# Issuing the matmuls that spread token weights over expert slots before the first expert's tile

## The chip, the cores and the metric

The kernel runs on one core of a Trainium2 chip as one program. The metric is device time in microseconds (us): 409.35 us is the median of three runs, which lie between 408.04 and 410.41 us. Engines are named as in the profile: PE is the matmul engine and PEld its loading of weights, DVE the vector engine, ACT the scalar engine, POOL the GpSimd engine and SP the engine that issues most transfers.

## The reference

Three layers follow each other: chunked attention, a gated feed-forward layer that mixes positions, and a mixture of eight experts. Only the last one matters here:

```
logits     = x @ w_gate                       # [B, S, 8]
e[b, s]    = argmax of logits, or the expert of the token before it (by a local gate)
p[b, s]    = softmax(logits[b, s])[e]
out[b, s]  = p * (relu(x[b, s] @ w1[e]) @ w2[e])
```

There are 2 x 768 tokens of width 512, and each expert has 512 x 1024 weights in w1 and 1024 x 512 in w2. The weight p multiplies the finished row of a token, so it is wanted only when a tile of outputs is scaled.

## The kernel before

Tokens are sorted into columns of 128 slots, and a column belongs to one expert. The columns form units: unit 0 is column 0 alone, five "pairs" hold two columns each, and singles of one column stand between them; two singles are kept in quarters or halves of a column (`PART`). One unit is one object of the class `Unit`. Its steps are `gather` (rows of x fetched by an indirect transfer on POOL into `xg`), `xt` (transposes on PE into `xgp`, split into a high part `xe_h` on ACT and a low part `xe_l` on DVE), `l1` (PE, into `hp`), `relu`, `l2` (PE, into `op`), `out` (ACT scales `op` by `psl` at line 1325, POOL stores it). A weight chunk of 128 x 512 is loaded by SP as `raw` and split by `conv` into `we_h` (ACT, some on DVE) and `we_l` (DVE, line 210). Each matmul product of two split operands takes three passes.

Routing ends with four products on PE. `inv` gives the token of every slot, `eps` (line 1074, `tile_experts`, token `RE`) the expert of every column, `inv0` the tokens of unit 0. The fourth is `slots5`: 36 matmuls (12 token tiles by 3 parts of the weight, lines 1047 to 1051) of a 128 x 128 matrix `m` of zeros and ones and `s_mp` of 23 columns sum into one bank `psl`, and ACT copies that bank to the table `psl` of weights by slot (line 1052). `part_in` (line 1056) copies two of its columns on DVE.

The order of work up to the first expert's tile is written out by hand: `ORDER` is a list of tokens, each naming a generator that issues one step when its token comes up, and all five engines keep that order. Behind it `moe.run` issues the experts, and there PE and SP keep the order in which the code issues, while a scheduler places the work of ACT, DVE and POOL. In `run` (line 1385) unit 0 comes first: `l1(0)`, `l1(1)` cut by `ht_s(0)`, `l2(0)`, `T[1].xt()`, `l2(1)`, then the hook `extra` (line 1424), then its outputs; from there a loop takes unit j's `l1` and unit j-1's `l2` in turn. `feed` keeps loads 31 chunks ahead of PE and conversions `LC` = 12 chunks ahead.

Ahead of unit 0, `xt_late` (token `XL`, line 1178) builds its `xgp` from eight gathered rows and sixteen late products and splits it at once; `xe_h` of that split is what unit 0's first matmul reads. Unit 0's passes are sorted so that the eight products with `xe_h` come first.

Of the kernel before, what the change touches and what calls it, by code (L numbers as in the profile page):

```python
# [94 lines left out]
x13m2 RP RA x04h0 RP RP RP x12.2 R3 x13m3 RA RA RP RP RP RA RL RP R4 RA x02h0 RA x04h1 x04.1 x04.2 x13.1 x02h1 x02.1  # L95
RP RP x13.2 RP r5 r5 x10m0 x10m1 x10m2 x10m3 x02.2 x10.1 x05h0 x05h1 x14m0 x14m1 x14m2 cm5 cm6 RP RP x05.1 r7 x03.2 RP
RA RA RZ RO RP RP x10.2 RZ RP RP RP x05.2 r1 r1 x14m3 x15m0 x14.1 RS RS x15m1 x15m2 r3 x14.2 RT RT x15m3 x15.1 RT G0
XL RT XL XL RT x15.2 cm7 r6 RE RE RP XL G1 G2 RA
""".split()

ENG = dict(
# [15 lines left out]
def tile_kernel(  # L117
# [269 lines left out]
    class Tr:  # L387
# [10 lines left out]
        def at(self, w, k, t0, n):  # L398
            g, o = divmod(t0, 256)
            return self.t[g, k // 2][w][:, (k % 2) * 256 + o : (k % 2) * 256 + o + n]  # L400
# [326 lines left out]
    RT = []  # L727
# [756 lines left out]
    moe = Moe([[0], *units, *singles[PU - 1 :]])  # L1484
# [86 lines left out]
    for name, fn, *a in (  # L1571
        ("R1", route1, 1, lx[1]), ("R2", route2, 1), ("R3", route3, 1), ("R4", route4, 1),
        ("RM", ranks_mm, 1), ("RA", rank_all), ("RP", place_ops), ("RZ", slots0), ("RS", slots3),
        ("RL", late_rows), ("RO", rows1, 1), ("RT", slots4), ("RE", tile_experts),
        ("G0", moe.T[0].gather, True), ("G1", moe.T[1].gather), ("G2", moe.T[2].gather),
        ("XL", lambda: (yield from moe.T[0].xt_late(xs[1][TT - LATE :]))),
    ):
        at(name, fn, *a)
    moe.extra, moe.later = slots5, {3: part_in, 5: part_out}

    live = {}

# [116 lines left out]
```

## Time and profile before

| | us |
|---|---|
| median of three runs | 409.35 |
| the profiled execution | 407.93 |
| its span from first to last instruction | 406.2 |
| PE busy | 394.1 (97% of the span) |
| DVE busy | 311.0 (77%) |
| ACT busy | 191.9 (47%) |
| POOL busy | 40.4 (10%) |

Times of a row are counted from the start of the span. A matmul's row has a start and a modelled end, and the starts of matmuls that follow each other lie closer together than a matmul is long (0.23 us against 0.39 us for 512 columns), so a matmul's price in a stream is the distance of two starts. In brackets behind a row stands the idle time of the engine ahead of it and who ended it.

### The profile page before, as it was taken

The page shows a single profiled execution, that of the slowest core. Times are in us where ns is not written, and L with a number is a line of the kernel's source. Part 1 is how long each engine was busy: PE and PEld are TensorE (multiplying, and loading weights), DVE is VectorE, ACT ScalarE, POOL GpSimd, SP SyncE. Part 2 cuts the span into 40 slices and gives each one's busy share as a digit, 9 for nine tenths or more (in the row PEclk, how much of TensorE's full clock was granted, in tenths as well). Part 3 has the DMA queues.
Part 4 walks back from the last instruction along what each step waited for, and adds up shares of the span by engine and source line. Part 5 has one row for each costly group of instructions (what it writes and reads, how often), then busy time and mean ns, then how long its engine had stood idle before and what let it go on. Part 6 is the DMA issues. An engine that isn't in the chain of part 4 may idle for free. (4 is left out here: it accounts for less than half of the span.)

```text
span 406.2 us, 9418 instructions
## 1 busy us (share of the span) xinstructions
PE 394.1 (97%) x3466; PEld 343.5 (85%) x3466; DVE 311.0 (77%) x749; ACT 191.9 (47%) x429; POOL 40.4 (10%) x58
## 2 busy tenths in 40 slices
PE   8979999999999999999999999999999999999994
PEld 4667899999999999996687789889888968978983
DVE  2989999999889988889799886996896684545400
ACT  4989885625454312520211265755683562643401
POOL 1000000020020010000000232101230210100201
PEclk9999999999999999999999999999999999999999
DMA  7999996100001032000074299999998599870101
GB/s 232 341 348 351 344 350 228 55 26 2 2 2 52 2 130 79 2 2 0 32 280 157 83 330 390 392 343 330 384 396 303 175 303 388 283 267 2 45 3 45
DMA packets 43703, 75.98 MB, mean 187 GB/s; under 512 B 5925, under 2 KB 12977, under 8 KB 43650
## 3 DMA queue, kind: packets, MB, share of 16 engines
q1 hardware_dynamic: 39682, 65.41, 46.8%
q0 software_dynamic: 2240, 6.75, 4.5%
q10 hardware_dynamic: 1728, 3.15, 2.0%
q8 instruction: 29, 0.48, 0.5%
q14 instruction: 24, 0.20, 0.2%
HBM read 68.99 MB, written 6.75 MB: 186 GB/s over the span
## 5 line engine op out<-in xcount | busy, mean ns | idle before, releaser
L210 DVE TENSOR_TENSOR we_l<-raw,we_h 128x512 fp32r<-128x512 f32 x128 | 82.1, 687 | 18.8 <-ACT we_h L205 18.1
L205 ACT ACTIVATE we_h<-raw 128x512 fp32r<-128x512 f32 x105 | 59.0, 625 | 17.2 <-DVE s_y L968 12.4
L1230 PE MATMUL hp<-xe_h,we_h 128*128 128x256 f32 x160 | 45.4, 284 | 0.0
L1230 PE MATMUL hp<-xe_h,we_l 128*128 128x256 f32 x160 | 44.9, 281 | 0.0
L1230 PE MATMUL hp<-xe_l,we_h 128*128 128x256 f32 x160 | 44.9, 281 | 0.0
L1313 PE MATMUL op<-we_h,ht_h 128*128 128x512 f32 x104 | 41.8, 402 | 0.0
L1313 PE MATMUL op<-we_l,ht_h 128*128 128x512 f32 x104 | 41.0, 394 | 0.0
L1313 PE MATMUL op<-we_h,ht_l 128*128 128x512 f32 x104 | 41.0, 394 | 0.0
L684 PE MATMUL vsp<-sg_h,vh_h 128*128 128x256 f32 x144 | 41.0, 285 | 0.0
L684 PE MATMUL vsp<-sg_l,vh_h 128*128 128x256 f32 x144 | 40.5, 281 | 0.0
L684 PE MATMUL vsp<-sg_h,vh_l 128*128 128x256 f32 x144 | 40.4, 280 | 0.0
L1230 PEld LDWEIGHTS hp<-xe_h,we_h 128*128 128x128 f32 x160 | 30.1, 188 | 0.1
L1230 PEld LDWEIGHTS hp<-xe_l,we_h 128*128 128x128 f32 x160 | 30.2, 188 | 0.0
L1230 PEld LDWEIGHTS hp<-xe_h,we_l 128*128 128x128 f32 x160 | 30.1, 188 | 0.0
L1262 DVE SCALAR_TENSOR_TENSOR ht_l<-hp,ht_h 128x512 fp32r<-128x512 f32 x20 | 13.8, 691 | 18.0 <-ACT ht_h L1261 18.0
L684 PEld LDWEIGHTS vsp<-sg_h,vh_h 128*128 128x128 f32 x144 | 27.1, 188 | 0.2 <-issue 0.2
L655 PE MATMUL ups<-x_h,in_h 128*128 128x256 f32 x96 | 27.2, 283 | 0.0
L684 PEld LDWEIGHTS vsp<-sg_h,vh_l 128*128 128x128 f32 x144 | 27.1, 188 | 0.0
L684 PEld LDWEIGHTS vsp<-sg_l,vh_h 128*128 128x128 f32 x144 | 27.1, 188 | 0.0
L655 PE MATMUL ups<-x_h,in_l 128*128 128x256 f32 x96 | 27.0, 281 | 0.0
L655 PE MATMUL ups<-x_l,in_h 128*128 128x256 f32 x96 | 27.0, 281 | 0.0
L469 ACT ACTIVATE a<-sc,nm 128x96 f32<-128x96 f32 x96 | 24.0, 385 | 2.5 <-DVE nm L466 2.5
(275 smaller groups left out, 930.5 us busy)
## 6 DMA issues: line engine op xcount, KB each, us to landing
raw<-in_w SPq DMA_DIRECT2D x160, 256.0 KB, 5.7
v<-in_vw SPq DMA_DIRECT2D x23, 260.0 KB, 5.3
k<-in_kw SPq DMA_DIRECT2D x24, 192.0 KB, 4.9
raw_in<-in_w_in SPq DMA_DIRECT2D x16, 256.0 KB, 5.6
q<-in_qT SPq DMA_DIRECT2D x12, 256.0 KB, 4.7
x1d<-x ACTq DMA_DIRECT2D x12, 256.0 KB, 2.1
rsg<-in_w_sgT SPq DMA_DIRECT2D x9, 256.0 KB, 4.4
raw_out<-in_w_out SPq DMA_DIRECT2D x8, 256.0 KB, 5.2
```

The lines of the kernel that those rows point to most:

```text
L205: nc.scalar.activation(hi, src, AF.Copy)
L210: nc.vector.tensor_tensor(lo, src, hi.bitcast(F32), ALU.subtract)
L469: nc.scalar.activation(self.a[:, j, :], sc[:, j, :], AF.Exp, bias=nm[:, j : j + 1])
L655: nc.tensor.matmul(ps[:, i * 256 : (i + 1) * 256], win_u[k][wa][:, f * 128 : (f + 1) * 128], xT[self.b].at(wb, k, 256 * self.g, 256), star ...
L684: nc.tensor.matmul(self.ps[:, h * 256 : (h + 1) * 256], self.vh[s].hl[wa][:, f * 128 : (f + 1) * 128], rhs_sg(wb, s, self.g), start=(s == ...
L1230: nc.tensor.matmul(ps[:, i * 256 : (i + 1) * 256], self.w[f // 4 * 4 + k][wa][:, f % 4 * 128 : (f % 4 + 1) * 128], self.x[k // 2][wb][:, k ...
L1262: nc.vector.scalar_tensor_tensor(l, self.ps[s], 0.0, h.bitcast(F32), ALU.max, ALU.subtract)
L1313: nc.tensor.matmul(self.po[c], h[wa][:, o : o + 128], self.w[8 + k][wb], start=(k == 0 and n == 0), stop=(k == 7 and n == 2),)
```

## The change

The token `R5` for `slots5` is entered in `ORDER` behind the last `XL` and ahead of `G1` and `G2`, the gathers of units 1 and 2, and the hook `extra` is no longer set. The 36 matmuls and the copy are the same ones.

```
-XL RT XL XL RT x15.2 cm7 r6 RE RE RP XL G1 G2 RA
+XL RT XL XL RT x15.2 cm7 r6 RE RE RP XL R5 G1 G2 RA
...
-        ("RL", late_rows), ("RO", rows1, 1), ("RT", slots4), ("RE", tile_experts),
+        ("RL", late_rows), ("RO", rows1, 1), ("RT", slots4), ("RE", tile_experts), ("R5", slots5),
...
-    moe.extra, moe.later = slots5, {3: part_in, 5: part_out}
+    moe.later = {3: part_in, 5: part_out}
```

On PE, between the last product of `eps` and unit 0's first matmul, stood before:

```order
L1074 MATMUL eps<-s_eqj,r0e 1x23
L1253 MATMUL hp<-we_h,xe_h 128x512
L1253 MATMUL hp<-we_l,xe_h 128x512
L1253 MATMUL hp<-we_h,xe_h 128x512
L1253 MATMUL hp<-we_l,xe_h 128x512
```

and the last of the 36 products stand there now:

```order
L1049 MATMUL psl<-s_mp_3675,m_3610 128x23
L1049 LDWEIGHTS m_3610
L1049 MATMUL psl<-s_mp_3676,m_3610 128x23
L1253 MATMUL hp<-we_h,xe_h 128x512
L1253 MATMUL hp<-we_l,xe_h 128x512
```

So all 36 have moved in between `eps` and `hp`.

On PE, between unit 0's `l2` and the first `l1` of unit 1 (`hp` with 256 columns), the end of the 36 stood before:

```order
L1049 MATMUL psl<-s_mp_3675,m_3610 128x23
L1049 LDWEIGHTS m_3610
L1049 MATMUL psl<-s_mp_3676,m_3610 128x23
L1230 MATMUL hp<-xe_h,we_h 128x256
L1230 MATMUL hp<-xe_l,we_h 128x256
```

and now `l2` meets `l1` directly:

```order
L1313 MATMUL op<-we_h,ht_h 128x512
L1313 MATMUL op<-we_l,ht_h 128x512
L1313 MATMUL op<-we_h,ht_l 128x512
L1230 MATMUL hp<-xe_h,we_h 128x256
L1230 MATMUL hp<-xe_l,we_h 128x256
```

On ACT, from the split of unit 0's `xgp` to the relu of unit 1's first `hp`, stood before:

```order
L205 ACTIVATE xe_h<-xgp 128x512
L205 ACTIVATE we_h<-raw 128x512 x3
L1266 ACTIVATE hr<-hp 128x512
L205 ACTIVATE ht_h<-htp 128x512
L205 ACTIVATE we_h<-raw 128x512 x3
L1266 ACTIVATE hr<-hp 128x512
L205 ACTIVATE ht_h<-htp 128x512
L205 ACTIVATE we_h<-raw 128x512 x3
L205 ACTIVATE xe_h<-xgp 128x512 x2
L1052 COPY psl<-psl 128x23
L205 ACTIVATE we_h<-raw 128x512 x2
L1261 ACTIVATE ht_h<-hp 128x512
```

and now:

```order
L205 ACTIVATE xe_h<-xgp 128x512
L1052 COPY psl<-psl 128x23
L205 ACTIVATE we_h<-raw 128x512 x3
L1266 ACTIVATE hr<-hp 128x512
L205 ACTIVATE ht_h<-htp 128x512
L205 ACTIVATE we_h<-raw 128x512 x3
L1266 ACTIVATE hr<-hp 128x512
L205 ACTIVATE ht_h<-htp 128x512
L205 ACTIVATE we_h<-raw 128x512 x3
L205 ACTIVATE xe_h<-xgp 128x512 x2
L205 ACTIVATE we_h<-raw 128x512
L1261 ACTIVATE ht_h<-hp 128x512
```

The copy has moved ahead of three conversions and the first `hr`. On DVE the two copies of `part_in` move with it:

```order
L210 TENSOR_TENSOR xe_l<-xgp,xe_h 128x512
L1056 COPY s_part<-psl 128x1 x2
L207 CAST we_h<-raw 128x512
L210 TENSOR_TENSOR we_l<-raw,we_h 128x512 x4
L210 TENSOR_TENSOR ht_l<-htp,ht_h 128x512
```

They now stand behind the `xe_l` of unit 0, where before they stood behind those of unit 1. POOL and SP issue the same instructions in the same order as before.

## Rows read from the trace of the kernel before

**Rows 1.** The page: engines' busy time; PE and its clock in 40 slices.
```profile
PE 394.1 (97%) x3466; PEld 343.5 (85%) x3466; DVE 311.0 (77%) x749; ACT 191.9 (47%) x429; POOL 40.4 (10%) x58
...
PE   8979999999999999999999999999999999999994
...
PEclk9999999999999999999999999999999999999999
```

**Rows 2.** Waits by engine and line over the span, PE's: total, times, longest.
```profile
PE xp L503 <- DMA v<-in_vw: 1.6, 3, 1.0
...
PE hp L1253 <- ACT xe_h L205: 0.3, 1, 0.3
```

**Rows 3.** Windows: stretch, length, busy time of PE, PEld, DVE, ACT, POOL; clock; DMA.
```profile
230.40:231.20 0.80, 0.50 (x14) 0.34 (x13) 0.52 (x3) 0.65 (x2) 0.00 (x0) 1.00 0.13 44
...
245.30:400.00 154.70, 154.70 (x1038) 133.25 (x1035) 97.27 (x168) 77.85 (x147) 23.93 (x23) 1.00 0.74 261
```

**Rows 4.** Timeline of PE at the end: start, us, instruction.
```profile
400.00 0.40 PE L1313 MATMUL op<-we_h,ht_l 128*128 128x512 f32 x1
```

**Rows 5.** Timeline of PE round the place where the products stand before.
```profile
244.11 0.39 PE L1313 MATMUL op<-we_h,ht_l 128*128 128x512 f32 x1
244.35 1.07 PE L1049 MATMUL psl<-s_mp,m 128*128 128x23 bf16 x36
245.27 0.36 PE L1230 MATMUL hp<-xe_h,we_h 128*128 128x256 f32 x1
245.47 0.28 PE L1230 MATMUL hp<-xe_l,we_h 128*128 128x256 f32 x1
245.59 0.28 PE L1230 MATMUL hp<-xe_h,we_l 128*128 128x256 f32 x1
```

**Rows 6.** Timeline of PE where one stream of products meets another.
```profile
263.40 0.40 PE L1253 MATMUL hp<-we_h,xe_l 128*128 128x512 f32 x1
263.64 0.40 PE L1313 MATMUL op<-we_h,ht_h 128*128 128x512 f32 x1
263.88 0.39 PE L1313 MATMUL op<-we_l,ht_h 128*128 128x512 f32 x1
```

**Rows 7.** Timeline of PE round the place where the products go.
```profile
230.44 0.45 PE L1074 MATMUL eps<-s_eqj,r0e 128*1 128x23 f16 x12
231.20 0.50 PE L1253 MATMUL hp<-we_h,xe_h 128*128 128x512 f32 x1 [0.30 <-ACT xe_h L205]
```

**Rows 8.** Timeline of DVE from the products' inputs to unit 1's split.
```profile
228.83 0.79 DVE L1040 TENSOR_TENSOR s_mp<-s_eqj,s_pp 128x276 bf16<-128x276 f16 x2
...
231.30 0.67 DVE L210 TENSOR_TENSOR xe_l<-xgp,xe_h 128x512 fp32r<-128x512 f32 x1
...
236.74 0.69 DVE L210 TENSOR_TENSOR ht_l<-htp,ht_h 128x512 fp32r<-128x512 f32 x1 [1.90 <-ACT ht_h L205]
...
243.69 1.28 DVE L210 TENSOR_TENSOR xe_l<-xgp,xe_h 128x512 fp32r<-128x512 f32 x2
245.66 0.21 DVE L1056 COPY s_part<-psl 128x1 f32<-128x1 f32 x2 [0.69 <-ACT psl L1052]
```

**Rows 9.** Timeline of ACT from unit 0's split to the copy and behind it.
```profile
230.55 0.60 ACT L205 ACTIVATE xe_h<-xgp 128x512 fp32r<-128x512 f32 x1 [0.60 <-PE xgp L1188]
231.04 1.66 ACT L205 ACTIVATE we_h<-raw 128x512 fp32r<-128x512 f32 x3
234.34 0.60 ACT L1266 ACTIVATE hr<-hp 128x512 f32<-128x512 f32 x1 [1.63 <-PE hp L1253]
...
245.45 0.18 ACT L1052 COPY psl<-psl 128x23 f32<-128x23 f32 x1 [2.82 <-PE psl L1049]
245.53 1.16 ACT L205 ACTIVATE we_h<-raw 128x512 fp32r<-128x512 f32 x2
248.41 0.60 ACT L1261 ACTIVATE ht_h<-hp 128x512 fp32r<-128x512 f32 x1 [1.73 <-PE hp L1230]
```

**Rows 10.** Waits of SP's queue over the span, at the loads of chunks.
```profile
SPq L1139 <- DMA raw<-in_w: 14.6, 24, 1.4
SPq L1139 <- DVE we_l L210: 11.7, 13, 6.3
```

## The prediction

> **What bounds the kernel now.** I read the page first: PE is busy for 97% of the span, with no slice but the last under 0.7, and its granted clock is full in all 40 slices [rows 1]. The next question is whether PE paces itself or waits. The waits of PE over the whole span are short, and only one lies near the change: unit 0's first matmul, which waits 0.3 us for `xe_h` [rows 2]. The windows agree: in the 0.80 us up to 231.20 PE is busy for 0.50 us, whereas from 245.30 to 400.00 it is busy for all 154.70 us [rows 3]. From there the chain runs through PE's last matmul, which starts at 400.00 [rows 4], then one scaling and one store, to the end at 406.2. So a microsecond that PE saves before 245 reaches the end, unless a smaller delay on ACT, DVE or SP comes to light behind it.
>
> **What is removed.** At the old place the 36 products start at 244.35 and the next matmul starts at 245.27: 0.92 us, or 0.026 us each [rows 5]. There is a second, smaller piece. The first matmul behind them takes 0.20 us to the next start, where the third comes 0.12 us after the second, so 0.08 us is lost where the bf16 products hand over to the split ones [rows 5]. Where one stream of split products meets another, the distance stays as it was: 263.40, 263.64, 263.88 [rows 6]. Without the 36, `l2` meets `l1` in that way, so I count the 0.08 us as gone too; by the other bound it stays. Removed: 0.92 to 1.00 us.
>
> **What is added.** At the new place the twelve `eps` products start at 230.44. Their row spans 0.45 us from the first start to the last end; at the spacing of the 36, 0.026 us, the next product could start at 230.44 + 12 x 0.026 = 230.75. The matmul that follows starts only at 231.20, since ACT's `xe_h` runs from 230.55 to 231.15 [rows 7, 9]. So 0.45 us of PE's time is free there (the 0.30 us in brackets is less because it counts from a modelled end). The 36 then run from 230.75 to 231.67, and unit 0 starts at 231.67 instead of 231.20: 0.47 us later. Its wait for `xe_h` is covered by the products, and what is late next is nothing on PE: `xe_l` ends at 231.97 [rows 8], and it is wanted only by the ninth matmul of unit 0, some two microseconds in. The handover of 0.08 us costs nothing new here, since `eps` already hands over to split products at this point.
>
> The inputs of the products are ready: the last two of the three `s_mp` end at 229.62 [rows 8], 1.1 us before PE gets there. If this cover were gone, PE would stand in front of unit 0 for as long as `s_mp` is late.
>
> **The sum on PE.** -1.00 + 0.47 = -0.53 us by the time unit 1's `l1` has passed the handover; -0.45 us if the handover stays.
>
> **What must hold between the two places.** Three chains run along unit 0, and each is moved by the change.
>
> ACT: the copy stands now ahead of three conversions. In the trace the copy starts 0.21 us after the start of the last product (245.27 - 0.03 = 245.24 to 245.45), and the conversion behind it 0.08 us after the copy [rows 5, 9]. So at the new place the copy starts at about 231.85, and the conversions at 231.93 instead of 231.04: 0.89 us late. What is queued behind is those three and `hr`, for which PE waits at its next transposes. ACT sat idle for 1.63 us before `hr` [rows 9], and `hr` itself is wanted 0.47 us later than before, so 1.63 + 0.47 - 0.89 = 1.2 us of cover is left, and nothing is paid. Further on ACT gains: the 2.82 us of waiting for the products, with two conversions queued behind, disappear [rows 9]. PE waits for no conversion there, so I count the gain at nothing; the most that it could be worth is a PE wait that no row shows.
>
> The Trainium skill ("TensorE: Matmul & The Clock Gate", section "Architectural detail: the array is 16× 32×32, not 1× 128×128") states that ACT and DVE take their queues strictly in order. That speaks against the change, since a copy that waits holds everything behind it. This trace agrees: the conversion at 245.53 stood behind the waiting copy [rows 9]. By the rule the hold is the 0.89 us above, and if ACT could pass a waiting instruction it would be nothing; with 1.2 us of cover left the sum is the same with both, and the rule decides only the rival below.
>
> DVE: the two `s_part` copies (0.21 us together) now stand ahead of a cast and four conversions and wait for ACT's copy until 232.1. They finish at about 232.3, where DVE before went on at 231.90. The 0.4 us are absorbed by the 1.90 us of idle time before `ht_l` at 236.74 [rows 8].
>
> DVE again, and here it is tight. From 236.74 to 244.97 DVE works without a gap, up to unit 1's two `xe_l` [rows 8]. This run starts with `ht_h`, which follows PE, so it shifts by PE's 0.47 us: the first `xe_l`, which ends at 243.69 + 0.68 = 244.37 (half of the pair's 1.28 us plus the overlap of two that follow each other), now ends at 244.84. ACT's `xe_h` releases PE 0.05 us after its end (231.15 to 231.20) [rows 7, 9]; by that PE may read `xe_l` from 244.89. PE itself now starts unit 1 at 244.35 + 0.47 = 244.82 and wants the first `xe_l` one matmul later, at 244.94. That leaves 0.05 us, and if the wait takes hold at the weights' load, which comes ahead of the matmul by about one distance of 0.12 us, PE is held by 0.07 us. So the gain lies between 0.45 and 0.53 us; I take 0.5.
>
> SP and POOL issue the same things in the same order. The loads of unit 1's chunks follow PE's releases by at most the 0.47 us, and conversions run twelve chunks ahead of PE: at 12 matmuls of 0.12 us to a chunk of a pair [rows 5] that is 17 us of work, and at three of 0.23 us to a chunk of a single [rows 6] it is 8 us.
>
> **Forecast.** 407.93 - 0.5 = 407.4 us against the profiled execution. That execution lies 1.42 us under the median of the runs shown; set on the median, the time is 409.35 - 0.5 = 408.85, say 408.8 us. That is 0.12%, far below the 0.5% (2.05 us) that a measurement of this kernel can tell from no change: its own three runs lie 2.37 us apart. The mechanism has 80% of my chance.
>
> **Rival 1: the gain is eaten before unit 1.** If the hold of ACT goes through to `ht_h` in full, DVE's unbroken run shifts by 0.89 us, the first `xe_l` ends at 245.26, and unit 1's second matmul can go at 245.31 instead of 245.47. The gain is then 0.16 us: 409.2 us. For it speaks that DVE has no gap in 8.2 us [rows 8]; against it, that 1.63 us of idle time lies ahead of `hr` and 1.90 us ahead of `ht_l` [rows 8, 9]. It would need a hold of over 2.1 us. The lower bound of this rival is no gain at all, 409.35, where the stall at 231.20 gives no cover. 12%.
>
> **Rival 2, slower: chunks come later.** The products' inputs are five buffers of the pool of 86 (two `m`, three `s_mp`) out of which every later chunk takes its buffer too. They come free 13.6 us earlier on PE, so the buffers are dealt out differently to the loads that follow, and such a load waits for whichever reader its buffer had last. In the trace the longest of these waits is 6.3 us, for a `we_l` [rows 10]. Two such waits in a row, 12.6 us, against the 8.4 us of conversions ahead at the singles would leave PE standing for 4.2 us: 409.35 - 0.5 + 4.2 = 413.05 us. It decides from about 8.4 us of lateness on. Against it: five buffers that come free earlier let loads go out earlier as a rule, and not one microsecond of PE behind 245.30 is idle [rows 3], so the stock of chunks never ran out. 4%.
>
> **Rival 3: more than the sum.** ACT's earlier conversions might let loads and later splits run ahead and take away short stalls that hide under the modelled ends of matmuls. Four such stalls of 0.5 us would be needed to get past 0.5%: 406.8 us. No row shows them. 4%.
>
> That the change doesn't do what it says is out: the order of instructions shows all 36 and the copy at the new place.
>
> **How the numbers follow.** Faster by over 0.5%: rival 3 and a little for scatter, 0.05. Slower by over 0.5%: rival 2 and a little for scatter, 0.05. Within: 0.90. The range is the forecast with the scatter of the runs shown, 1.3 us below their median and 1.1 us above, and reaches rival 1: 407.3 to 410.4 us. Rival 2 lies outside it.
>
> **What would show it.** In the changed profile `psl` should run from about 230.75 to 231.67 with no wait before unit 0's first `hp`; that `hp` should start about 1.2 us after the first `eps`, not 0.76 us; `l2` of unit 0 should meet unit 1's `hp` with no 0.08 us of handover; ACT's `hr` should still have idle time before it; and from unit 1's first matmul to PE's last the distance should be the 154.7 us of before. The prediction is wrong if that distance changes by over half a microsecond, if PE waits for `xe_l` or for a chunk behind unit 0, or if the products are slower than 0.026 us each at their new place.

## The result, and the profile after

The changed kernel takes 412.25 us (median of six runs, 410.98 to 413.45) where the kernel before takes 408.94 (six runs, 408.04 to 410.41): a ratio of 1.0073, 95% interval 1.0050 to 1.0096. It is slower by about 3 us. The forecast was 408.8 us, and 412.25 lies outside its range of 407.3 to 410.4. The profiled execution of the changed kernel takes 411.96 us, with a span of 410.2.

The page's rows for PE and its clock, which answer to [rows 1]: as many busy microseconds as before, at full clock, in a longer span.

```profile
PE 394.2 (96%) x3466; PEld 343.0 (84%) x3466; DVE 311.0 (76%) x749; ACT 192.5 (47%) x429; POOL 40.4 (10%) x58
...
PE   8888999999999999999999989899999999999994
...
PEclk9999999999999999999999999999999999999998
```

So PE waits. Its waits by line (total, times, longest) now hold two behind 230 us that [rows 2] don't have, and the wait for `xe_h` at unit 0 is gone:

```profile
PE op L1313 <- ACT ht_h L205: 1.6, 1, 1.6
PE hp L1253 <- DVE xe_l L210: 1.3, 1, 1.3
```

The windows (stretch, length, busy time of PE and the others) answer to [rows 3]. The new place is filled; the 5.2 us round unit 0's first `op` hold 1.64 us of idle time; and from unit 1's first matmul to PE's last there are 156.43 us instead of 154.7, with 1.25 us idle.

```profile
230.76:232.06 1.30, 1.30 (x49) 1.25 (x49) 1.02 (x5) 0.60 (x1) 0.00 (x0) 1.00 0.06 19
236.00:241.20 5.20, 3.56 (x16) 2.07 (x15) 1.07 (x2) 2.12 (x5) 1.90 (x2) 1.00 0.91 282
247.73:404.16 156.43, 155.18 (x1035) 133.27 (x1033) 97.65 (x168) 77.08 (x145) 23.96 (x23) 1.00 0.72 253
```

PE's timeline at the new place and at the old one (start, duration, instruction; answers to [rows 5, 7]):

```profile
230.76 0.45 PE L1074 MATMUL eps<-s_eqj,r0e 128*1 128x23 f16 x12
231.14 1.07 PE L1049 MATMUL psl<-s_mp,m 128*128 128x23 bf16 x36
232.06 0.48 PE L1253 MATMUL hp<-we_h,xe_h 128*128 128x512 f32 x1
...
247.50 0.40 PE L1313 MATMUL op<-we_h,ht_l 128*128 128x512 f32 x1
247.73 0.28 PE L1230 MATMUL hp<-xe_h,we_h 128*128 128x256 f32 x1
247.85 0.35 PE L1230 MATMUL hp<-xe_l,we_h 128*128 128x256 f32 x1
248.04 0.29 PE L1230 MATMUL hp<-xe_h,we_l 128*128 128x256 f32 x1
```

The products went where they should and cost what they should. The loss begins behind them. PE's and ACT's timelines of the changed kernel:

```profile
236.48 0.66 PE L1279 MATMUL htp<-ident,hr 128*128 128x128 f32 x4
236.89 0.48 PE L1253 MATMUL hp<-we_h,xe_h 128*128 128x512 f32 x1
237.21 0.39 PE L1253 MATMUL hp<-we_l,xe_h 128*128 128x512 f32 x1
237.44 1.07 PE L1253 MATMUL hp<-we_h,xe_l 128*128 128x512 f32 x4
240.15 0.51 PE L1313 MATMUL op<-we_h,ht_h 128*128 128x512 f32 x1 [1.64 <-ACT ht_h L205]
```
```profile
235.83 0.60 ACT L1266 ACTIVATE hr<-hp 128x512 f32<-128x512 f32 x1 [1.81 <-PE hp L1253]
239.50 0.60 ACT L205 ACTIVATE ht_h<-htp 128x512 fp32r<-128x512 f32 x1 [3.08 <-PE hp L1253]
```

The four transposes `htp` end at 237.14, ACT is idle, and nothing stands ahead of `ht_h`; still it starts only at 239.50. In the kernel before, `ht_h` starts at 236.11 behind transposes that end at 236.08:

```profile
235.48 0.60 PE L1279 MATMUL htp<-ident,hr 128*128 128x128 f32 x4
```
```profile
236.11 0.60 ACT L205 ACTIVATE ht_h<-htp 128x512 fp32r<-128x512 f32 x1 [1.17 <-PE htp L1279]
```

In the changed trace PE's semaphore for these transposes is updated at 239.476, and the three updates behind it follow at 239.52, 239.55 and 239.60, though the matmuls that they belong to started at 237.21, 237.44 and 238.12. PE had worked; its reports came late and in a bunch. SP's queue too took 0.73, 0.69 and 0.73 us over three instructions between 237.21 and 239.40; instructions of these kinds take 0.05 to 0.46 us at that place of the kernel before. What runs on POOL then are gathers, first in the changed kernel, then in the kernel before:

```profile
234.88 0.95 POOL L1176 DMA_INDIRECT xg<-x1d,gidx  x1 [0.30 <-issue]
236.14 0.95 POOL L1176 DMA_INDIRECT xg<-x1d,gidx  x1 [0.30 <-issue]
237.39 0.95 POOL L1176 DMA_INDIRECT xg<-x1d,gidx  x1 [0.30 <-issue]
```
```profile
236.01 0.95 POOL L1176 DMA_INDIRECT xg<-x1d,gidx  x1 [0.30 <-PE hp L1253]
237.26 0.95 POOL L1176 DMA_INDIRECT xg<-x1d,gidx  x1 [0.30 <-issue]
```

The last two (unit 3's, the fourth and fifth of a row of five) start 0.53 us behind the first transpose in the kernel before, and 0.34 us ahead of it in the changed one. Counted from the first `eps` product the transposes have moved back by 0.69 us (5.03 to 5.72), and the fourth gather has come forward by 0.19 us (5.57 to 5.38).

The second stall is of the same make. Unit 1's third `ht_h` (line 1261) waits 3.21 us for PE, while unit 4's and 5's gathers run; `xe_h` and `xe_l` of unit 2 stand behind it on ACT and DVE, and PE waits for the latter. ACT, POOL and DVE of the changed kernel:

```profile
258.99 0.60 ACT L1261 ACTIVATE ht_h<-hp 128x512 fp32r<-128x512 f32 x1 [3.21 <-PE hp L1230]
259.48 0.62 ACT L205 ACTIVATE we_h<-raw 128x512 fp32r<-128x512 f32 x1
260.00 0.59 ACT L205 ACTIVATE xe_h<-xgp 128x512 fp32r<-128x512 f32 x1
```
```profile
255.21 0.98 POOL L1176 DMA_INDIRECT xg<-x1d,gidx  x1 [0.30 <-issue]
256.50 0.99 POOL L1176 DMA_INDIRECT xg<-x1d,gidx  x1 [0.30 <-issue]
257.79 0.94 POOL L1176 DMA_INDIRECT xg<-x1d,gidx  x1 [0.30 <-issue]
```
```profile
261.89 0.68 DVE L210 TENSOR_TENSOR xe_l<-xgp,xe_h 128x512 fp32r<-128x512 f32 x1
```

Where the time went, as the distance in us from the first `eps` product to PE's start of each step (the last column is an experiment below, the changed kernel with five gathers held back):

| PE starts | before | changed | changed, both holds |
|---|---|---|---|
| unit 0's first hp | 0.76 | 1.31 | 1.31 |
| unit 0's first htp | 5.03 | 5.72 | 5.55 |
| unit 0's first op | 6.86 | 9.39 | 7.38 |
| unit 1's first hp | 14.82 | 16.97 | 14.41 |
| unit 2's first hp | 27.54 | 29.89 | 27.07 |
| the op behind it | 33.20 | 37.10 | 32.72 |
| the last matmul | 169.56 | 173.40 | 169.07 |

### The profile page after: what moved, and what is told of

Its sections match the earlier page's. It is cut to its first block, busy times and chain, and to the rows that moved or that the text cites. A ratio compares the mean times of both kernels' runs of the same rounds, so it can differ in the third digit from the quotient of the medians.

```text
span 410.2 us, 9414 instructions
## 1 busy us (share of the span) xinstructions
PE 394.2 (96%) x3466; PEld 343.0 (84%) x3466; DVE 311.0 (76%) x749; ACT 192.5 (47%) x429; POOL 40.4 (10%) x58
## 5 line engine op out<-in xcount | busy, mean ns | idle before, releaser
L1313 PEld LDWEIGHTS op<-we_h,ht_h 128*128 128x128 f32 x104 | 19.5, 188 | 7.5 <-ACT ht_h L205 2.1
```

Source lines behind the costliest of these rows:

```text
L1313: nc.tensor.matmul(self.po[c], h[wa][:, o : o + 128], self.w[8 + k][wb], start=(k == 0 and n == 0), stop=(k == 7 and n == 2),)
```

## The experiments

Several theories were put to the test. **G**: POOL's gathers hold up PE's reports for one to two microseconds, and the change moves unit 0's transposes into such a stretch. **S**: the five slot buffers that come free early re-deal the buffers of loads and gathers. **A1** and **A2** (or P): ACT's copy in front of unit 0, or the products themselves. Ratios are to the kernel before on the same chip, with 95% intervals.

**The two kernels once more.**

> The changed kernel once more, to see whether its two stalls of PE (1.8 us before unit 0's first op matmul at 238.1, 1.3 us before a pair's hp at 261.0) stand at the same places in another execution. Theory A (the change itself makes PE report finished matmuls late near unit 0, so that ACT's ht_h starts 2 to 3 us late and PE waits for it): time 411 to 413 us, both stalls again at the same instructions, ACT's ht_h again over 2 us behind the end of the transposes. Theory B (the profiled execution was disturbed, and the loss sits elsewhere): time still 411 to 413 us, but the stalls stand at other instructions or are missing. Theory C (there is no real loss): time within 0.5% of the kernel before, 407 to 411 us.

> The kernel before, profiled once more. Theory A: 408 to 410 us, PE without a wait of 0.5 us or more between 231 and 400 us, and ACT's ht_h of unit 0 within 0.7 us of the start of its transposes. Theory B: stalls of one to two microseconds turn up in this profile as well, at some place between 231 and 400 us.

The changed kernel: 411.70 us, ratio 1.0062 (1.0028 to 1.0096); both stalls at the same instructions (0.67 instead of 0.23 us between two starts at `op`, 1.3 us at `xe_l`). Theory A holds for the time and the places. `ht_h` was not over 2 us late as it had said: it starts 1.28 us behind the last transpose's start, where the first profile has 2.64. So the first stall varies in size. The kernel before: 408.19 us, ratio 0.9990 (0.9958 to 1.0023). Its `ht_h` at unit 0 is on time, but its profile does hold a late report, at the second place, which theory A had not expected: PE waits 0.55 us there, and loses 0.83 us between unit 2's first `hp` and the next `op` (6.49 instead of 5.66). ACT and POOL of that run:

```profile
256.03 0.60 ACT L1261 ACTIVATE ht_h<-hp 128x512 fp32r<-128x512 f32 x1 [2.81 <-PE hp L1230]
```
```profile
252.88 0.94 POOL L1176 DMA_INDIRECT xg<-x1d,gidx  x1 [0.30 <-issue]
254.13 0.95 POOL L1176 DMA_INDIRECT xg<-x1d,gidx  x1 [0.30 <-issue]
```

So the trace on which the prediction rested showed the kernel before in an execution in which this place went well.

**The copy issued from the old place; then products at both places.**

```
-        nc.scalar.copy(psl, ps)           # in slots5
+        R["psl_ps"] = ps                  # the copy itself from the hook extra
```
```
-XL RT XL XL RT x15.2 cm7 r6 RE RE RP XL G1 G2 RA
+XL RT XL XL RT x15.2 cm7 r6 RE RE RP XL R5 G1 G2 RA
...
+        ("R5", spare5),                   # 36 products into a bank nobody reads
```

> The changed kernel, but only the 36 products stand at the new place; ACT's copy of their bank to psl stays where it was before, behind unit 0's second l2. Theory A1 (the loss comes from ACT's queue: the copy ahead of the conversions holds ACT in order and shifts unit 0's and unit 1's splits): the stalls are gone and the time is 408 to 409.5 us. Theory A2 (the loss comes from PE: the products or their bank just ahead of unit 0): the stalls stay and the time is 411 to 413 us.

> The kernel before with everything at its old place, and in addition a second set of the 36 products into a bank that nobody reads, at the new place. By the prediction's own prices it costs 0.47 us: 409.8 us. Theory A1 (ACT's copy at the new place is the cause): 409.5 to 410.2 us, no stall. Theory A2 (the products or the turn of the six banks just ahead of unit 0 are the cause): unit 0's ht_h late by over 2 us, a stall before op, 412 to 414 us.

The first of the two runs took 412.15 us, ratio 1.0084 (1.0052 to 1.0117), with the stall before `op` in full. But its copy did not stay at the old place. The code issues it from the hook, and behind `ORDER` a scheduler places ACT's work; it put the copy where the changed kernel has it. ACT's row of it in this run, in which the first `eps` starts at 230.60:

```profile
232.11 0.18 ACT L1055 COPY psl<-psl 128x23 f32<-128x23 f32 x1 [0.81 <-PE psl L1049]
```

That is 1.51 us behind `eps`, as in the changed kernel, and the copies of `part_in` follow on DVE at 1.72 us in both. So this run is the changed kernel over again, and it decides nothing on A1.

With products at both places the copy does stand at its old place (15.55 us behind `eps`): 410.08 us, ratio 1.0032 (1.0003 to 1.0062), no stall before `op`, and PE's last matmul 0.55 us later than in the repeated kernel before (170.96 against 170.41 from the first `eps`). That is the price of the new place. It speaks against A2 as it was put, and it is what A1 had expected. A1 falls only by runs further down, in which copy and products stand at the new place and the stall is gone. ACT's `ht_h` and POOL's fourth gather in the one and in the other:

```profile
239.19 0.60 ACT L205 ACTIVATE ht_h<-htp 128x512 fp32r<-128x512 f32 x1 [3.58 <-PE hp L1256]
...
235.97 0.95 POOL L1179 DMA_INDIRECT xg<-x1d,gidx  x1 [0.30 <-issue]
```
```profile
236.49 0.60 ACT L205 ACTIVATE ht_h<-htp 128x512 fp32r<-128x512 f32 x1 [1.17 <-issue]
...
235.87 0.94 POOL L1185 DMA_INDIRECT xg<-x1d,gidx  x1 [0.30 <-issue]
```

Transposes start at 236.15 and at 235.86, so the fourth gather comes 0.18 us ahead of them in the first and 0.01 us behind them in the second. In both, unit 0 starts 1.31 us behind `eps`; what differs at the transposes is the gathers, 0.19 us earlier in the first.

The traces tell where these 0.19 us begin: at the end of the row's second gather. POOL in the kernel before (first `eps` at 230.44) and in the changed one (230.76):

```profile
233.44 1.01 POOL L1176 DMA_INDIRECT xg<-x1d,gidx  x1 [0.30 <-issue]
```
```profile
233.45 1.12 POOL L1176 DMA_INDIRECT xg<-x1d,gidx  x1 [0.30 <-issue]
```

It ends 4.01 us behind `eps` in all six profiles with the copy at the old place, and at 3.81 to 3.82 us in all eight with it at the new, wherever it starts (2.57 to 3.00 us). Both times this is 0.30 us behind the start of one of DVE's conversions (3.71 and 3.52 us), and DVE's order there has changed with the copies of `part_in`. The third to fifth gather follow at fixed distances unless they are held. So the copy, through DVE's order, seems to bring the gathers forward; no run moves the copy alone, and this is not shown.

**The buffers held back.**

```
+    def hold():                           # as the hook extra, three products
+        for i, tt in enumerate((0, TT, TT)):
+            nc.tensor.matmul(ps, m1[tt], mp[i][:, tt, :], start=(i == 0), stop=(i == 2))
```

> The changed kernel with three small products at the old place that read the five buffers (two m, three s_mp) into a bank nobody reads, so that these buffers come free as late as in the kernel before. Theory S (the five buffers that come free early re-deal the loads' and gathers' buffers, and that makes the stalls): the first stall before unit 0's op goes, POOL's second gather of the run stands again 3.0 us behind the first eps product and not 2.7, time 408.5 to 410 us. Theory G (POOL's fourth and fifth gather hold up PE's reports of finished matmuls for some two microseconds, and the change moves unit 0's first transposes into that stretch): the stall goes if the gathers move back by 0.25 us with the buffers, and stays at 1.5 to 2 us, 411 to 413 us in all, if they don't. Theory P (the products just ahead of unit 0 themselves): stall stays, 411 to 413 us.

411.93 us, ratio 1.0073 (1.0036 to 1.0111). The stall stays, with all five buffers released late: theory S falls for the stall. The second gather stayed at 2.7 us behind `eps` and the fourth at 5.36, so the buffers are not what brings the gathers forward either, and G, which then expected the stall to stay, is neither hurt nor proved.

**Unit 3's gathers held back, in the changed kernel and in the kernel before.**

```
+                nc.gpsimd.tensor_tensor(warm[:, 0:1], a, a, ALU.subtract)   # in gather: a is a column of after
...
             if n > 3:
-                T[3].gather()             # ahead of unit 0's l1
+                T[3].rows()               # only takes the buffers
...
+            if n > 3:
+                T[3].gather(after=(T[1].x[1] or T[1].x[0])[0])   # behind T[1].xt()
```

> The changed kernel with the two gathers of unit 3 held back on POOL until unit 1's second xe_h is there (a one-column operation on POOL reads it), some 6 us later than before; the buffers are dealt as in the changed kernel. Theory G: PE's reports are on time at unit 0's transposes, the stall before op (0.4 to 1.9 us) is gone, the second stall, before a pair's hp near 261 us, stays, time 409.3 to 410.3 us. Theories S and P: the stall before op stays and the time is 411 to 413 us.

> The kernel before with unit 3's two gathers held back in the same way. Theory G: nothing was hit at unit 0 in the kernel before, so nothing is won there, 408 to 409.5 us; the later gathers stand closer to unit 4's and to unit 0's store, which may cost up to 1 us. Theories S and P: the same, 408 to 409.5 us. The run prices the hold by itself.

The changed kernel falls to 409.13 us, ratio 0.9989 (0.9959 to 1.0020), just under what G expected and far from the other theories. Copy and products stand at the new place here, so A1 and A2 fall too: neither is enough for the stall. The gathers start at 242.96 and 244.65, and `ht_h` follows its transposes (first one at 235.19) at once:

```profile
235.83 0.60 ACT L205 ACTIVATE ht_h<-htp 128x512 fp32r<-128x512 f32 x1 [1.23 <-PE htp L1287]
```

The kernel before with the same hold: 410.67 us, ratio 1.0025 (0.9991 to 1.0058), so the hold by itself wins nothing; the median lies 1.2 us above the expectation's upper end. In both profiles the second place then costs 3.1 us (8.76 and 8.74 us from unit 2's first `hp` to `op`). Windows of the changed kernel with the hold (PE busy, and the clock third from the end) show how a wait there grows:

```profile
258.00:260.00 2.00, 0.75 (x3) 0.49 (x3) 1.97 (x5) 2.00 (x5) 0.00 (x0) 1.00 1.03 384
260.00:262.00 2.00, 2.00 (x6) 1.57 (x5) 2.00 (x4) 2.00 (x5) 0.00 (x0) 0.53 1.05 384
262.00:264.00 2.00, 2.00 (x7) 1.58 (x6) 1.97 (x5) 2.00 (x5) 0.00 (x0) 0.62 1.00 358
```

PE was idle for 1.25 of the first 2.00 us (and for 0.53 us just before them, up to 257.46), and behind that the granted clock fell from 1.00 to 0.5 (1.2 of 2.4 GHz) for 3.4 us.

**Two spare sets in the kernel before.**

```
+        ...                               # the 36 products of spare5 a second time
```

> The kernel before with the products at their old place and two spare sets of 36 products (into a bank nobody reads) ahead of unit 0, so that unit 0 starts about 1.4 us later than before against POOL's gathers, which don't wait for it. One spare set gave 410.08 us and no stall before op. Theory G: the transposes now fall into the stretch of the fourth and fifth gather: ht_h comes over 1 us late, a stall before op of 1 to 2.4 us, time 412 to 413.5 us. Theories S and P-with-copy: no stall before op, 410.08 + 0.92 = 411.0 us.

413.49 us, ratio 1.0088 (1.0059 to 1.0118), against 1.0032 with one set: some 2.3 us more (the medians, on two chips, lie 3.4 us apart), where the second set's own price is 0.92. In a kernel whose real products, copy and buffers are all at their old places the stall can thus be made by delay alone, of 1.46 us; the 0.55 us of one set, which is also the change's own delay, did not make it. It sits one step earlier than G had put it, since unit 0 is now so late that it is the report of its first `hp` (whose last products end at 235.25) that meets the gathers at 235.59 and 236.84. ACT's `hr` and PE's transposes:

```profile
239.04 0.60 ACT L1280 ACTIVATE hr<-hp 128x512 f32<-128x512 f32 x1 [6.76 <-remote]
240.38 0.60 ACT L205 ACTIVATE ht_h<-htp 128x512 fp32r<-128x512 f32 x1 [0.75 <-PE htp L1293]
```
```profile
239.69 0.66 PE L1293 MATMUL htp<-ident,hr 128*128 128x128 f32 x4 [3.04 <-ACT hr L1280]
```

**Plain transfers for the gathers.**

```
-                T[3].gather()
+                T[3].plain()              # for each i, c: nc.gpsimd.dma_start(self.xg[c], x1d[1 + 128 * i : 129 + 128 * i, :])
```

> The changed kernel, unit 3's two gathers replaced by two plain transfers of the same size from POOL, of 128 rows that follow each other (unit 3 then works on other rows than the reference wants). Theory G1 (the gather's indirect form holds up PE's reports): the stall before op goes, 409 to 410 us. Theory G2 (the bytes of the transfers beside the chunk loads do it, whatever the form): the stall stays, 411 to 413 us.

410.87 us, ratio 1.0038 (1.0018 to 1.0059). The stall before `op` is gone, though the two transfers are issued 0.47 us ahead of the first transpose, right where gathers hurt. POOL and ACT:

```profile
235.63 1.19 POOL L1181 DMA_DIRECT2D xg<-x1d  x2
```
```profile
236.74 0.60 ACT L205 ACTIVATE ht_h<-htp 128x512 fp32r<-128x512 f32 x1 [1.17 <-PE htp L1284]
```

The same bytes in plain form do no harm here, as G1 said of the stall; the time is 0.9 us over G1's upper end. POOL is busy with two of them for 1.19 us instead of 2.2, so the form and the time that it takes on POOL were changed together, and which of the two matters is not shown. The second place cost its 3.1 us in this profile too, and that is why the time stays above 410. The Trainium skill ("DMA: Bandwidth & Descriptors", section "SWDGE vs HWDGE vs iDMA") says that transfers issued from GpSimd, direct and indirect, have their descriptors built in software on that engine. The section makes no difference between the two forms; at unit 0 of this run they differ (`ht_h` 0.31 us behind the last transpose's start with plain transfers, 1.28 to 2.64 us in the changed kernel's two profiles).

**The second place.**

```
-                            if j + 3 < n:
+                            if 1 < j < n - 3:
                                 T[j + 3].gather()
...
                         if s == 0 and j == 1 and n > 2:
                             T[2].xt()
+                            if n > 4:
+                                T[4].rows()
+                                T[4].gather(after=T[2].x[0][1])   # a POOL operation reads unit 2's xe_l first
```

> The changed kernel with only the second hold (unit 4's gather behind unit 2's xe_l); unit 3's gathers stand where they stood. Theory G: the stall before unit 0's op stays at 0.4 to 2 us, the one before a pair's hp near 261 us goes, 409.5 to 411.5 us. Theory N: both stay, 411 to 413 us.

> The changed kernel with two holds on POOL: unit 3's gathers wait for unit 1's second xe_h (as in the run before), and unit 4's gather, with unit 5's two in order behind it, for unit 2's xe_l, so that no gather stands between 251 and 257 us, where PE's reports were late and the second stall followed. Theory G: both stalls gone, PE without a wait over 0.5 us between 231 and 270 us; against the 409.13 us with one hold another 0.8 to 3 us is won (the second stall with half the clock behind it took 3.1 us of that profile): 406 to 408.3 us. Theory N (the second stall has nothing to do with gathers, it is the run of DVE): the stall stays near 261 us, 408.5 to 410 us.

> The kernel before with the same two holds. Theory G: 406.5 to 408.8 us, and the distance to the changed kernel with both holds is the change's price where no gather interferes: by the prediction's sum 0.5 us less for the changed kernel. Theory N: 408.5 to 411 us.

In these three runs the POOL operation writes into the gather's own buffer, where the one above wrote into `warm`. With the second hold alone: 409.07 us, ratio 1.0020 (0.9999 to 1.0042), 0.4 us under theory G's lower end; the stall before `op` stays (0.68 us), the one at 261 is gone (5.66 us). With both holds the changed kernel takes 407.30 us, ratio 0.9965 (0.9945 to 0.9985). It is faster than the kernel before and than the changed one, and PE has no idle time in the 70 us that held both stalls:

```profile
230.00:300.00 70.00, 70.00 (x447) 61.60 (x444) 57.87 (x101) 45.31 (x86) 18.14 (x18) 1.00 0.99 355
```

The kernel before with both holds: 407.91 us, ratio 0.9991 (0.9976 to 1.0006). The intervals of the two kernels overlap, so the times alone don't tell them apart. In the two profiles PE's last matmul starts 169.07 and 169.54 us behind the first `eps`: the change wins 0.47 us where no gather interferes. Theory N falls.

Unit 0 in the traces: the fourth gather's start against that of the first transpose, `ht_h` behind the last transpose's start, and the distance of `op` from the matmul ahead of it (us):

| kernel | 4th gather | ht_h | op |
|---|---|---|---|
| before; the same again | +0.53; +0.52 | 0.31; 0.31 | 0.24; 0.23 |
| products at both places | +0.01 | 0.31 | 0.23 |
| changed with one hold; with both | +7.8; +7.9 | 0.31; 0.31 | 0.24; 0.24 |
| before with one hold; with both | +7.9; +7.9 | 0.31; 0.31 | 0.23; 0.24 |
| changed again; with the second hold | -0.17; -0.17 | 1.28; 1.30 | 0.67; 0.68 |
| changed, copy issued from the hook | -0.18 | 2.71 | 2.10 |
| changed with buffers held; changed | -0.33; -0.34 | 2.58; 2.64 | 1.95; 2.03 |

Every kernel of the table whose fourth gather starts ahead of the transposes has the stall before `op`, and none of the others has it. Two runs are not in it: with two spare sets the gathers stand 4.1 us ahead of the transposes and the stall stands before these, and with plain transfers, 0.47 us ahead, there is none.

## Why the prediction was wrong

The **sum on PE** was right. Added: forecast 0.47, measured 0.55 (1.31 against 0.76), because the first product starts 0.39 us behind the first `eps` and not 0.31; the 36 take 0.92 us as said. Removed: from unit 0's last stretch of `op` to unit 1's first `hp` there are 2.85 us instead of 3.78, so 0.93 of the forecast 0.92 to 1.00. The handover's 0.08 us was won: the first step at 247.73 is short now (0.12 us). But the next takes 0.19 us, and this looks like the hold of 0.07 us that the paragraph on DVE's tight `xe_l` allowed for: that `xe_l` ends 0.02 to 0.04 us behind unit 1's first matmul in the profiles of the changed kernel (0.02 was forecast), and where `l2` meets `l1` with `xe_l` long there, at 379.85, all steps take 0.12 us. Net, with the gathers held in both kernels, -0.47 us, inside the forecast -0.45 to -0.53.

The **wait for `xe_h`** was covered, as said, and **ACT's hold** did no harm by itself: `hr` still has 1.81 us of idle time before it, and with the gathers held back `ht_h` follows its transposes at 0.31 us although the copy stands at the new place. Rival 1 is thus out in the form it had, and so is rival 2: PE's waits name no chunk. The lower end of the range, 407.3, lies 0.2 us under what its own terms give (408.8 - 1.3 = 407.5); at 412.25 this decides nothing.

The **step that failed** is "SP and POOL issue the same things in the same order", which I priced at nothing. The order is the same; the time against PE is not. POOL's gathers don't wait for unit 0: the fourth stands 5.57 us behind the first `eps` in the kernel before and 5.56 with a spare set ahead of unit 0. In the changed kernel unit 0 moves back by 0.55 us, the gathers come forward by 0.19 (5.38), and the transposes of its first profile stand another 0.14 us late. So a distance of 0.53 us turned into -0.34. The delay of 0.55 us was in the sum (as 0.47), and alone it left 0.01 us and no stall; the 0.19 us were nowhere in it, and what brings them about was not tested (the experiment with products at both places says what points to DVE). With the distance fell the unspoken assumption of the ACT paragraph that `ht_h` follows PE's transposes at 0.31 us. The first stall costs 1.84 us between `htp` and `op` and 0.55 us more up to unit 1 (beside the 0.93 us that the products give back there), since `ht_l` and the next transposes stand behind it. The second costs 1.55 us in the profiled execution (7.21 against 5.66); there the kernel before is hit in part of its executions as well, and what the changed kernel loses more at that place, from run to run, these profiles don't settle. Of the signs named under "would be wrong if" two showed the second stall: the distance from unit 1 to the end, 156.43 instead of 154.7 us, and a wait of PE for `xe_l` (1.3 us). None of them covered the first, which stands ahead of unit 1.

Rows that I had read told half of it: SP and POOL were read for order and for what they wait, and no row of POOL's timeline was set beside PE's.

## What to carry to other kernels

A step that is moved on one engine changes its distance to everything that doesn't wait for it. Set the timelines of POOL's indirect transfers beside the tight handovers from PE to ACT and back, before and after the move, and not only the order on each engine. Here the gathers' place was worth more than the edit itself: with two of them moved the changed kernel's ratio went from 1.0062 to 0.9989, and with three more to 0.9965.

An edit in the code is not yet a move on the chip. Where a scheduler places an engine's work, look in the experiment's own trace for the instruction that was to move or to stay, before its time is read as an answer.

## What the runs showed of the hardware

- PE's semaphore updates came 0.4 to 3.7 us behind the ends of its matmuls, in bunches some 0.04 us apart, while POOL's indirect gathers ran next to chunk loads that kept the DMA engines over 80% busy (3.7 us with two spare sets: 235.25 to 238.96). Without loads the delay was smaller: in four profiles an indirect store of POOL near the end, with a DMA share of 0.00 beside it, went with an update 0.7 to 0.8 us late (368.48 to 369.25 in the changed kernel). ACT's and DVE's updates were not late by over 0.3 us in any trace. Most traces lack some of these records (15 of ACT's 377 in the changed kernel), so this holds for those that are there.
- The large delays stand at the fourth and fifth gather of a row and at those behind unit 0's store. The first two of the row run before the loads have filled the DMA engines (none of their time is busy from 232 to 233 us in the kernel before). Whether the loads are needed for the large delays wasn't tried, and by which path a gather holds up PE stays open. So does the jump of `ht_h` from 1.3 to 2.7 us between gathers 0.17 and 0.18 us ahead, and why the second place is hit in some executions and not in others.
- In five of the fourteen profiles waits of PE behind 230 us were followed by 3.4 us at half the granted clock: one wait of 3.04 us, and four times a wait of 0.5 to 0.7 us and one of 1.25 us within 2 us. Behind the single waits of 1.56 to 1.71 us there the clock stayed full.
